# Scattering the token rows themselves into the experts' lists, in place of a list of token numbers

## The chip, the cores and the metric

The kernel runs on one core of a Trainium2 chip. The metric is the device time of one execution in microseconds (us); below it, "the time" is the median of several executions. Engines are named as the profile names them: PE (TensorE, matmuls and transposes), DVE (VectorE), ACT (ScalarE), POOL (GpSimd), SP (SyncE, which here only issues transfers). [...]

## The reference

Three stages follow each other over N = 3072 tokens of width 512 (4 batches of 768 positions, 8 heads of 64):

```python
a = softmax(where(sink(4 keys) | window(128), q @ k.T / 8, -1e9))      # per batch and head
x = (a @ v) regrouped to [3072, 512]
e = argmax(x @ w_gate + modality_bias[modality_id])                     # one of 8 experts a token
y[t] = softmax(...)[e] * (relu(x[t] @ w1[e]) @ w2[e])                   # w1[e] 512x1024, w2[e] 1024x512
out = max(y @ m_w1, y @ m_w2, y @ m_w3) @ m_wo                          # dense, hidden width 768
```

All arithmetic is float32; products are made from a high and a low part (three matmuls for each product of the second and third stage).

## The kernel before

**Attention, 24 blocks of 128 tokens.** The function `beat(g)` writes one eighth of a block's steady state: block n, beat h of 8. The order of every engine's instructions is the order in which they are written; each engine runs its own list in order, and an instruction whose inputs are not ready holds up all that stand behind it on the same engine. In each second beat PE transposes the probabilities of two heads (`flip_p`, L464), ACT copies them to `pT` (L469), POOL cuts them with two selects into `pc` and `pb` (`part_p`, L480), and four beats later PE multiplies them with v (`av`, L513 and L517). So POOL stands on PE's way, with some beats of slack.

**Routing.** Two blocks later the row of x is complete; block n - 3 is routed in beat h = 3 of block n. `place` (L605) works out on DVE the place of each of the 128 tokens in its expert's list (`rowi`: expert number times 3072 plus rank) and POOL scatters the 128 token numbers, 4 bytes each, to these places of the DRAM list `ids` (L617). `store` (L592) puts the gate's factor in column 512 of x (the token number is in column 513, L542) and SP stores the 128 rows of 2056 bytes in token order to the DRAM tensor `xd` (L597). The two chains are woven on DVE, one instruction of each in turn. Every scatter writes `ids` at places that are not known when the program is made, so each waits until the one before it has landed, and every gather of `ids` waits for the last scatter.

**Slots.** The experts' work is cut into slots of 256 tokens of one expert, two halves x of 128 each. The first four slots are chosen from the counts while attention is running (`pick`, L682, one instruction or two a beat; `DONE` = 16, 18, 20, 22 blocks done); the rest are laid out by `tables` (L740) once all counts are known, its steps spread over slot 1, with one large product on POOL (`dots`, L792). A slot's tokens come in two steps: `tokens` (L817) gathers 128 token numbers from `ids` by `idxi` into `tk`, and when these have landed `rows` (L824) gathers the 128 rows of `xd` by `tk` into `xgt`. Both are issued by POOL. For the picked slots `tokens` stands at the end of `pick`; later ones are gathered just ahead of `rows`. Then PE transposes `xgt` (`flip_slot`, L857), multiplies with w1 (L876), ACT and DVE make `hh`, `hl`, and PE multiplies with w2 (L925). Weights come in two tiles of 512 KB by SP each; ACT and DVE split them (`whi` L845, `wlo` L848). `keep_down` (L929) scales the product on DVE into `ytl`, and POOL scatters 128 rows of 2052 bytes to `yd` (L932), each again waiting for the one before.

**Filling work in the slots.** The dense stage's weights arrive as float64 and are converted on DVE in eight steps (`convert`, L639) with a sum on POOL (L663); the next conversion's first step (L647) overwrites what this sum reads.

**Tail and dense stage.** Slots from number 11 on (`tail_slot`, L1345, `last_slot`, L1377) stand under run-time conditions and use `grid`, `masks` and the two `ytl` tiles as scratch (L913), so that ACT waits there until the scatters out of `ytl` have landed. The dense stage (L1464, L1480) follows and keeps PE alone busy.

POOL's list at the end of attention and in slot 1, in order: scatter of block 21, scatter of block 22, `tokens(3)`, first `yd` scatter of slot 0, `rows(2)`, scatter of block 23, second `yd` scatter, `rows(3)`, `dots`, the `yd` scatters of slot 1. In a later slot: two `meta` copies, `tokens`, `rows`, a conversion's sum and store, the two `yd` scatters.

Of the kernel before, what the change touches and what calls it, by code (L numbers as in the profile page):

```python
# [9 lines left out]
F32 = mybir.dt.float32  # L10
F32R = mybir.dt.float32r
BF16 = mybir.dt.bfloat16
I32 = mybir.dt.int32
# [6 lines left out]
P = 128  # L20
# [22 lines left out]
def kernel(  # L43
# [32 lines left out]
    cst = ctx.enter_context(tc.tile_pool(name="cst", bufs=1))  # L76
    drm = ctx.enter_context(tc.tile_pool(name="drm", bufs=1, space=DRAM))

    xd = drm.tile([NT, DM + 2], F32, name="xd")
    yd = drm.tile([NT + SLOT, DM + 1], F32, name="yd")  # L80
    ids = drm.tile([E * NT, 1], I32, name="ids")
    xg = drm.tile([B, S, H, D], F32, name="xg")
    wa = drm.tile([JC, P, 3 * CC * P], F32, name="wa")
    wb = drm.tile([JC, P, DM], F32, name="wb")
# [2 lines left out]
    def iota(shape, pattern, base, mult, name):  # L87
        t = cst.tile(shape, F32, name=name)
        nc.gpsimd.iota(t, pattern=pattern, base=base, channel_multiplier=mult, allow_small_or_imprecise_dtypes=True)
        return t  # L90
# [10 lines left out]
    xgt = [wp.tile([P, DM + 2], F32, name=f"xgt{x}") for x in range(2)]  # L101
    ytl = [wp.tile([P, DM + 1], F32, name=f"ytl{x}") for x in range(2)]
    meta = [[wp.tile([P, 2], F32, name=f"meta{u}{x}") for x in range(2)] for u in range(2)]
    tk = [[wp.tile([P, 1], I32, name=f"tk{u}{x}") for x in range(2)] for u in range(2)]
    xh = wp.tile([P, CC, SLOT], F32R, name="xh")
    xl = wp.tile([P, CC, SLOT], F32R, name="xl")
    hh = wp.tile([P, FC, SLOT], F32R, name="hh")
# [186 lines left out]
        additive_p(mk1, tb[:, 0:4])  # L294

    ltri = cst.tile([P, P], BF16, name="ltri")
    tokid = cst.tile([P, NTILE], I32, name="tokid")
    tokf = cst.tile([P, NTILE], F32, name="tokf")
    zid = mn.tile([P, E * NT // P], I32, name="zid", bufs=1)
    vr = mn.tile([P, B, D], F32, name="vr", bufs=1)  # L300
    bmask = mn.tile([P, H, D], F32, name="bmask", bufs=1)
    prow = cst.tile([P, 1], I32, name="prow")
# [289 lines left out]
    def store(n):  # L592
        s = st[n]
        nc.vector.tensor_scalar(s.gs, s.gs, 1.0e-9, None, ALU.add)
        yield
        nc.vector.reciprocal(s.x[:, DM:DM + 1], s.gs)
        nc.sync.dma_start(xd[n * P:(n + 1) * P, :], s.x)  # L597

    def rank(n):
        s = st[n]  # L600
# [4 lines left out]
    def place(n):  # L605
        s = st[n]
        pos = lt.tile([P, E], F32, name="pos", tag="pos")
        row = lt.tile([P, 1], F32, name="row", tag="row")
        nc.vector.tensor_add(pos, s.pr[:, 0, :], cnt)
        yield  # L610
        nc.vector.tensor_tensor_reduce(
            out=pos, in0=pos, in1=s.oh, scale=1.0, scalar=0.0, op0=ALU.mult, op1=ALU.add, accum_out=row,
        )
        nc.vector.tensor_add(cnt, cnt, s.pr[:, 1, :])
        yield
        nc.vector.tensor_copy(rowi[:, n:n + 1], row)
        nc.gpsimd.indirect_dma_start(  # L617
            out=ids, out_offset=bass.IndirectOffsetOnAxis(ap=rowi[:, n:n + 1], axis=0),
            in_=tokid[:, n:n + 1], in_offset=None,
        )  # L620


    cv = {}
# [58 lines left out]
    def pick(z):  # L682

        c, t = pick_t
        m, w, o = pick_s
        V = nc.vector
        V.tensor_tensor(c, cnt, base_e, ALU.subtract)
        if z:
            V.tensor_tensor(c, c, taken, ALU.subtract)
        yield  # L690
        V.reduce_max(m, c, axis=AX.X)
        yield
        V.scalar_tensor_tensor(t, c, m, wdesc, ALU.is_ge, ALU.mult)
        yield
        V.reduce_max(w, t, axis=AX.X)
        yield
        V.tensor_scalar(pick_oh[z], t, w, None, ALU.is_equal)
        V.tensor_scalar(w, w, -1.0, float(E), ALU.mult, ALU.add)
        yield
        V.tensor_copy(esi[:, z:z + 1], w)  # L700
        V.tensor_scalar(w, w, float(NT), pcol, ALU.mult, ALU.add)
        if z:
            V.tensor_tensor_reduce(
                out=t, in0=taken, in1=pick_oh[z], scale=1.0, scalar=0.0, op0=ALU.mult, op1=ALU.add, accum_out=o
            )
        yield
        if z:
            V.tensor_add(w, w, o)
            yield
        V.tensor_copy(idxi[:, z, 0:1], w)  # L710
        V.tensor_scalar(idxi[:, z, 1:2], w, float(P), None, ALU.add)
        if z:
            V.scalar_tensor_tensor(taken, pick_oh[z], float(SLOT), taken, ALU.mult, ALU.add)
        else:
            V.tensor_scalar(taken, pick_oh[z], float(SLOT), None, ALU.mult)
        for x in range(2):
            yield
            tokens(z, x)

    E2 = 2 * E  # L720
    cnt_e = cst.tile([P, E], F32, name="cnt_e")
# [18 lines left out]
    def tables():  # L740
# [62 lines left out]
        for x in range(2):  # L803
            if x:
                V.tensor_scalar(seff, seff, float(P), None, ALU.add)
            V.tensor_add(idx[:, :, x], dot[:, :, 1], seff)
            V.scalar_tensor_tensor(pos2[:, :, x], dot[:, :, 2], float(PICKS * SLOT), seff, ALU.add, ALU.add)
            V.tensor_tensor(padi[:, :, x], seff, dot[:, :, 3], ALU.is_ge)
        V.tensor_copy(idxi[:, PICKS:, :], idx)
        yield  # L810

        for x in range(2):
            V.tensor_scalar(padi[:, :, x], padi[:, :, x], padn[:, x:x + 1], None, ALU.mult)
        V.tensor_tensor(pos2, pos2, padi, ALU.max)
        V.tensor_copy(posi[:, PICKS:, :], pos2)

    def tokens(s, *only):  # L817
        for x in only or range(2):
            nc.gpsimd.indirect_dma_start(
                out=tk[s % 2][x], out_offset=None, in_=ids,  # L820
                in_offset=bass.IndirectOffsetOnAxis(ap=idxi[:, s, x:x + 1], axis=0),
            )

    def rows(s, upto=None, only=(0, 1)):  # L824
        for x in only:
            nc.gpsimd.indirect_dma_start(
                out=xgt[x], out_offset=None, in_=xd[0:upto] if upto else xd,
                in_offset=bass.IndirectOffsetOnAxis(ap=tk[s % 2][x], axis=0),
            )

    def fetch(s, half, only=range(4)):
# [105 lines left out]
    def weave(*chains):  # L937

        chains = list(chains)
        first = chains[0] if chains else None  # L940
        todo = 0
        while chains:
            todo %= len(chains)
            if next(chains[todo], chains) is chains:
                chains.pop(todo)
            else:
                todo = 0 if todo == 1 and chains[0] is first else todo + 1
# [21 lines left out]
    def beat(g):  # L969
# [63 lines left out]
            if 0 <= c < NCV and x == min(t * CVG // 8, CVG - 1):  # L1033
                chains.append(once(convert, c, t, cvt[c % 2], nc.sync))
        if gone and h == 3:
            chains += [place(n - 3), store(n - 3)]
        if sunk and h == 1:
            chains.append(sink_split(n - 1))
        if prev and h == 4:
# [16 lines left out]
    if True:  # L1056
# [16 lines left out]
        nc.gpsimd.affine_select(  # L1073
            out=ltri, in_=ltri, pattern=[[1, P]], compare_op=ALU.is_gt, fill=0.0, base=0, channel_multiplier=-1
        )
        nc.gpsimd.memset(zid, 0)
        nc.gpsimd.dma_start(ids.rearrange("(p n) o -> p (n o)", p=P), zid)
        nc.gpsimd.iota(prow, pattern=[[0, 1]], base=0, channel_multiplier=1)
        nc.gpsimd.iota(
            bmask, pattern=[[1, H], [0, D]], base=0, channel_multiplier=0, allow_small_or_imprecise_dtypes=True  # L1080
# [2 lines left out]
        base_e = iota([P, E], [[NT, E]], 0, 0, "base_e")  # L1083
        pcol = iota([P, 1], [[0, 1]], 0, 1, "pcol")
        padn = iota([P, 2], [[P, 2]], NT, 1, "padn")
        siota = iota([P, RS], [[1, RS]], 0, 0, "siota")
        kiota = iota([P, SMIN], [[SLOT, SMIN]], 0, 0, "kiota")
        nc.gpsimd.iota(tokid, pattern=[[P, NTILE]], base=0, channel_multiplier=1)
        nc.gpsimd.iota(
            tokf, pattern=[[P, NTILE]], base=0, channel_multiplier=1, allow_small_or_imprecise_dtypes=True  # L1090
        )
# [17 lines left out]
        for g in range(LAST + 1):  # L1109
            beat(g)  # L1110
            n, h = divmod(g, H)
            for z in range(PICKS):
                if n == DONE[z] + 2 and h == 6 + (z == 0):
                    picking.append(pick(z))
            if picking and next(picking[-1], 0) == 0:
                picking.pop()
            if (n, h) in FIRST:
                fetch(0, 0, (FIRST.index((n, h)),))
            if n == DONE[0] + 4 and h in (5, 7):
                rows(0, DONE[0] * P, (h // 2 - 2,))  # L1120

            if (n, h) in HI:
                split_hi(*piece(HI.index((n, h))))
            if (n, h) in LO:
                x = LO.index((n, h))
                split_lo(*piece(x), eng=None if x % 4 else nc.gpsimd.tensor_sub)
            if n == 23:
                if h in (0, 2):
                    px[h // 2] = flip_slot(0, h // 2, ps_tr, "tr")
                if h in (1, 3):  # L1130
                    keep_slot(h // 2, px[h // 2])
                    keep_slot_lo(h // 2, px[h // 2])
                if h == 6:
                    rows(1, DONE[1] * P)
                if h == 7:
                    fetch(1, 0)
    mctx.close()
# [63 lines left out]
    keep_down(0, py, meta[0][0], posi[:, 0, 0:1])  # L1201
    py = ps_av.tile([P, DM], F32, name="py", tag="av")
    down(1, 0, py, lambda: rank(n - 1))
    rows(2, DONE[2] * P)
    split_lo(2)
    split_hi(3)
    weave(place(n - 1), store(n - 1))
    split_lo(3)
    down(1, 1, py)
    keep_down(1, py, meta[0][1], posi[:, 0, 1:2])  # L1210
# [74 lines left out]
    def next_rows(s):  # L1285

        px = [flip_slot(s, x, ps_x, "px") for x in range(2)]
        for x in range(2):
            keep_slot(x, px[x])
            keep_slot_lo(x, px[x])  # L1290
        if s >= SMIN - 1:
            for x in range(2):
                nc.gpsimd.tensor_copy(metal[x], meta[s % 2][x])
            nc.gpsimd.tensor_copy(posl, posi[:, s, :])
        if s + 1 < SMAX:
            if s + 1 >= PICKS:
                tokens(s + 1)
            rows(s + 1)

    def slot(s):  # L1300
# [21 lines left out]
        if s + 1 >= SMIN - 1:  # L1322
            for x in range(2):
                nc.gpsimd.tensor_copy(metal[x], meta[(s + 1) % 2][x])
            nc.gpsimd.tensor_copy(posl, posi[:, s + 1, :])
        if s + 2 >= PICKS:
            tokens(s + 2)
        rows(s + 2)
        for x in range(2):
            py = ps_y.tile([P, DM], F32, name="py", tag="py")  # L1330
# [226 lines left out]
```

## Time and profile before

| | |
|---|---|
| time, median of 3 runs | 1054.43 us (1048.15 to 1061.04) |
| the profiled execution | 1054.27 us, span 1052.7 us, mean granted clock 0.973 |
| PE busy | 994.5 us (94% of the span) |
| DVE busy | 583.2 us (55%) |
| ACT busy | 395.9 us (38%) |
| POOL busy | 322.3 us (31%) |
| hardware queue of SP and ACT | 111.68 MB, 43.1% of the DMA engines' span |
| POOL's own queue | 25.08 MB, 7.1% |

Busy time is an average over four stages: attention to about 290 us, a passage into the slots to about 345 us, slots to about 560 us, the tail to about 640 us, and the dense stage. Matmuls are pipelined and their ends are modelled, so a PE that is shown busy throughout can still run at less than its rate; its real pace is read from the starts of successive instructions. A number in square brackets behind a row of the timeline is the idle time of the engine before this instruction, with the event that the profile holds to have ended it.

### The profile page before, as it was taken

To read this page: it belongs to the slowest core of one execution; us is meant where nothing else is said; L and a number is where in the kernel's file an instruction comes from. 1 tells how busy PE (TensorE), PEld (TensorE's weight loads), DVE (VectorE), ACT (ScalarE), POOL (GpSimd) and SP (SyncE) were. 2 spreads that over 40 slices of the span, in tenths; PEclk is the share of its full clock that TensorE was granted. 3 is DMA by queue.
4 is the path that set the end of the run, shared out by engine and by line. 5 is a ranking of instruction groups with operands and counts; after the bars stand their busy time and mean duration, and the time that the engine had idled before them with its cause. 6 is when DMAs were issued, how large, how long until landed. Compare 5 with 4: busy or idle time off the path is not lost. (4 is left out here: it accounts for less than half of the span.)

```text
span 1052.7 us, 16293 instructions
## 1 busy us (share of the span) xinstructions
PE 994.5 (94%) x5621; PEld 857.2 (81%) x5621; DVE 583.2 (55%) x1312; ACT 395.9 (38%) x974; POOL 322.3 (31%) x503
## 2 busy tenths in 40 slices
PE   6998999998998999989999779999999999999997
PEld 4898988987887998979988657888888888888885
DVE  3787886886767897969898354512302213122120
ACT  3665564565553444434445343411111111111111
POOL 4444434435525454434555450010010000100001
PEclk8998998999999999999999889999999999999999
DMA  7494999666478889787988544210100101100001
GB/s 148 108 123 103 155 124 140 141 118 144 95 205 239 258 293 286 231 283 224 312 262 297 180 135 140 90 50 21 31 40 21 41 21 31 50 13 18 30 1 41
DMA packets 134081, 137.96 MB, mean 131 GB/s; under 512 B 85888, under 2 KB 95248, under 8 KB 133984
## 3 DMA queue, kind: packets, MB, share of 16 engines
q1 hardware_dynamic: 124464, 111.68, 43.1%
q0 software_dynamic: 9376, 25.08, 7.1%
q8 instruction: 49, 0.80, 0.3%
q14 instruction: 48, 0.39, 0.2%
q10 hardware_dynamic: 144, 0.00, 0.0%
HBM read 117.19 MB, written 25.87 MB: 136 GB/s over the span
## 5 line engine op out<-in xcount | busy, mean ns | idle before, releaser
L1464 PE MATMUL pa<-yh,wah 128*128 128x512 f32 x432 | 170.9, 396 | 0.0
L1464 PE MATMUL pa<-yh,wal 128*128 128x512 f32 x432 | 169.9, 393 | 0.0
L1464 PE MATMUL pa<-yl,wah 128*128 128x512 f32 x432 | 169.6, 393 | 0.0
L848 DVE TENSOR_TENSOR wlo<-wraw,whi 128x1024 fp32r<-128x1024 f32 (+1 forms) x110 | 143.8, 1314 | 13.3 <-ACT whi L845 12.9
L1469 DVE TENSOR_TENSOR mm<-pa,mm 128x512 f32<-128x512 f32 x36 | 24.9, 691 | 193.2 <-PE pa L1464 193.2
L845 ACT CAST whi<-wraw 128x1024 fp32r<-128x1024 f32 (+1 forms) x116 | 114.3, 1022 | 21.8 <-PE py L925 17.3
L876 PE MATMUL ph<-xh,wlo 128*128 128x256 f32 x352 | 102.2, 290 | 6.1 <-DVE wlo L848 6.1
L426 PE MATMUL sc<-kT,qz 128*128 128x260 f32 (+1 forms) x384 | 102.3, 391 | 4.8 <-POOL qz L359 3.7
L876 PE MATMUL ph<-xh,whi 128*128 128x256 f32 x352 | 101.5, 288 | 0.0
L876 PE MATMUL ph<-xl,whi 128*128 128x256 f32 x352 | 101.4, 288 | 0.0
L1471 ACT CAST dh<-mm 128x512 fp32r<-128x512 f32 x36 | 22.4, 621 | 197.7 <-DVE mm L1470 197.7
L1464 PEld LDWEIGHTS pa<-yh,wal 128*128 128x128 f32 x432 | 81.1, 188 | 18.4
L1464 PEld LDWEIGHTS pa<-yl,wah 128*128 128x128 f32 x432 | 81.2, 188 | 17.9
L1464 PEld LDWEIGHTS pa<-yh,wah 128*128 128x128 f32 x432 | 81.1, 188 | 17.7
L1484 POOL DMA_INDIRECT out_dram<-ot,ti x24 | 23.3, 973 | 207.7 <-ACT ot L1483 207.7
L925 PE MATMUL py<-whi,hh 128*128 128x512 f32 x208 | 84.5, 406 | 0.7 <-DVE hl L904 0.3
L925 PE MATMUL py<-whi,hl 128*128 128x512 f32 x208 | 82.1, 395 | 0.0
L925 PE MATMUL py<-wlo,hh 128*128 128x512 f32 x208 | 82.0, 394 | 0.0
L426 PEld LDWEIGHTS sc<-kT,qz 128*128 128x128 f32 x384 | 67.8, 200 | 12.0 <-POOL qz L359 4.2
L452 ACT ACTIVATE pp<-sc,m 128x132 f32<-128x132 f32 (+1 forms) x192 | 70.6, 372 | 11.4 <-DVE m L445 10.7
L876 PEld LDWEIGHTS ph<-xh,wlo 128*128 128x128 f32 x352 | 68.3, 194 | 6.8 <-DVE wlo L848 6.8
L513 PE MATMUL av<-vn,pb 128*128 128x64 f32 x320 | 60.0, 270 | 11.0 <-POOL pb L480 8.6
(269 smaller groups left out, 2095.8 us busy)
## 6 DMA issues: line engine op xcount, KB each, us to landing
wraw<-in_moe_w_dram SPq DMA_DIRECT2D x119, 512.0 KB
xd<-x SPq DMA_DIRECT2D x24, 257.0 KB
yn<-yd SPq DMA_DIRECT2D x24, 256.5 KB
kn<-in_k_dram SPq DMA_DIRECT2D x24, 256.0 KB
qn<-in_q_dram SPq DMA_DIRECT2D x24, 256.0 KB
vn<-in_v_dram SPq DMA_DIRECT2D x24, 256.0 KB
x<-xg ACTq DMA_DIRECT2D x24, 256.0 KB
cvr<-in_moe_w_dram SPq DMA_DIRECT2D x11, 512.0 KB
```

What stands on the lines that cost most here:

```text
L426: nc.tensor.matmul(ps[:, o, :w], s.qT[:, h + o, :], kT[:, c, a:a + w], start=True, stop=True)
L452: nc.scalar.activation(s.p[:, h, :w], s.sc[h // 2][:, h % 2, :w], AF.Exp, bias=s.m[:, h:h + 1], scale=1.0, accum_out=s.sum[:, h:h + 1],)
L513: nc.tensor.matmul(s.av[:, h, :], back_p[:, h % 2], st[n - 1].v[:, h, :], start=(h == 0), stop=False, skip_group_check=True,)
L845: (eng or nc.scalar.copy)(whi[c][:, o], wraw[c][:, o])
L848: (eng or nc.vector.tensor_sub)(wlo[c][:, o], wraw[c][:, o], whi[c][:, o].bitcast(F32))
L876: nc.tensor.matmul(ph[:, g, :], a[:, fs], m[:, c, :], start=(n == 0 and g == 0), stop=(n == 3 * CC - 1), skip_group_check=True,)
L925: nc.tensor.matmul(py, a[:, f, hs], m[:, ws], start=(f == 0 and i == 0), stop=(f == FC - 1 and i == 2))
L1464: nc.tensor.matmul(ps, a[:, sl], m[:, c, :], start=(n == 0), stop=(n == 3 * CC - 1))
L1469: nc.vector.tensor_tensor(m, pa[1], m, ALU.max)
L1471: nc.scalar.copy(dh[:, j, :], m)
L1484: nc.gpsimd.indirect_dma_start(out=out, out_offset=bass.IndirectOffsetOnAxis(ap=ti[g % 2][:, t:t + 1], axis=0), in_=o, in_offset=None,)
```

## The change

Rows of x no longer lie in `xd` in token order. `xd` grows to 24576 rows of 514 words (8 lists of 3072), and POOL scatters each block's 128 rows of 2056 bytes straight to `rowi`, in place of SP's store. The list `ids`, its zeroing at the start, its scatter, the tiles `tk` and every gather of `tokens` are gone; `rows` gathers from `xd` by `idxi`. `place` and `store` are one chain, `place_store`, so the scatter stands behind the reciprocal. Since the rows now read all of `xd`, the bounds that `rows` had (only the blocks that are done) are gone; `rows(0)` moves from beats 5 and 7 of block 20 to beats 0 and 2 of block 21. The list's unused places hold nothing now, so `tables` sends the indices of a slot's missing tokens back to its first row, with two more DVE instructions and one more step. Block 22's place is worked out where it was, but its scatter stands where its store stood, behind the end of `pick(3)`.

```diff
-    xd = drm.tile([NT, DM + 2], F32, name="xd")
+    xd = drm.tile([E * NT, DM + 2], I32, name="xd")
-    ids = drm.tile([E * NT, 1], I32, name="ids")
...
         nc.vector.reciprocal(s.x[:, DM:DM + 1], s.gs)
-        nc.sync.dma_start(xd[n * P:(n + 1) * P, :], s.x)
+        nc.gpsimd.indirect_dma_start(
+            out=xd, out_offset=bass.IndirectOffsetOnAxis(ap=rowi[:, n:n + 1], axis=0),
+            in_=s.x.bitcast(I32), in_offset=None,
+        )
...
         nc.vector.tensor_copy(rowi[:, n:n + 1], row)
-        nc.gpsimd.indirect_dma_start(
-            out=ids, out_offset=bass.IndirectOffsetOnAxis(ap=rowi[:, n:n + 1], axis=0),
-            in_=tokid[:, n:n + 1], in_offset=None,
-        )
+
+    def place_store(n):
+        yield from place(n)
+        yield
+        yield from store(n)
...
-        for x in range(2):
-            yield
-            tokens(z, x)
...
+        yield
+
+        for x in range(2):
+            V.scalar_tensor_tensor(
+                idx[:, :, x], padi[:, :, x], back[:, x:x + 1], idx[:, :, x], ALU.mult, ALU.add
+            )
         V.tensor_copy(idxi[:, PICKS:, :], idx)
...
-    def tokens(s, *only):
-        for x in only or range(2):
-            nc.gpsimd.indirect_dma_start(
-                out=tk[s % 2][x], out_offset=None, in_=ids,
-                in_offset=bass.IndirectOffsetOnAxis(ap=idxi[:, s, x:x + 1], axis=0),
-            )
-
-    def rows(s, upto=None, only=(0, 1)):
+    def rows(s, only=(0, 1)):
         for x in only:
             nc.gpsimd.indirect_dma_start(
-                out=xgt[x], out_offset=None, in_=xd[0:upto] if upto else xd,
-                in_offset=bass.IndirectOffsetOnAxis(ap=tk[s % 2][x], axis=0),
+                out=xgt[x].bitcast(I32), out_offset=None, in_=xd,
+                in_offset=bass.IndirectOffsetOnAxis(ap=idxi[:, s, x:x + 1], axis=0),
             )
...
         if gone and h == 3:
-            chains += [place(n - 3), store(n - 3)]
+            chains.append(place_store(n - 3))
...
-        nc.gpsimd.memset(zid, 0)
-        nc.gpsimd.dma_start(ids.rearrange("(p n) o -> p (n o)", p=P), zid)
...
+        back = iota([P, 2], [[-P, 2]], 0, -1, "back")
...
-            if n == DONE[0] + 4 and h in (5, 7):
-                rows(0, DONE[0] * P, (h // 2 - 2,))
+            if n == DONE[0] + 5 and h in (0, 2):
+                rows(0, (h // 2,))
...
-    weave(place(n - 1), store(n - 1))
+    weave(place_store(n - 1))
...
         if s + 1 < SMAX:
-            if s + 1 >= PICKS:
-                tokens(s + 1)
             rows(s + 1)
...
-        if s + 2 >= PICKS:
-            tokens(s + 2)
         rows(s + 2)
```

## Rows read from the trace of the kernel before

**Rows 1.** Busy time by stage: PE, PEld, DVE, ACT, POOL, clock, DMA share, GB/s.

```profile
345.00:560.00 215.00, 207.42 (x1351) 190.45 (x1350) 186.31 (x263) 99.40 (x131) 100.61 (x113) 0.98 0.84 266
560.00:640.00 80.00, 68.31 (x294) 52.81 (x293) 43.58 (x47) 34.62 (x45) 38.35 (x47) 0.91 0.56 179
```

**Rows 2.** Waits of all engines: who waited for whom, us in total, times, longest.

```profile
DVE cvt L647 <- POOL cvt L663: 20.3, 5, 8.6
...
POOL vs L370 <- DMA ids<-tokid,rowi: 18.8, 3, 7.8
...
PE av L513 <- POOL pb L480: 8.6, 5, 2.7
```

**Rows 3.** Groups of POOL's instructions: busy us, mean ns | idle before them, what ended it.

```profile
L826 POOL DMA_INDIRECT xgt<-xd,tk x30 | 35.8, 1193 | 55.3 <-DMA tk<-ids,idxi 36.3 <-PE py L925 5.2 <-PE px L1258 4.1
...
L819 POOL DMA_INDIRECT tk<-ids,idxi x30 | 33.3, 1112 | 35.2 <-DVE cnt_e L744 11.6 <-DVE x L596 6.6 <-DMA ids<-tokid,rowi 6.3
```

**Rows 4.** PE's timeline, four of its stalls: start, us, instruction, idle before.

```profile
239.84 0.43 PE L513 MATMUL av<-vn,pb 128*128 128x64 f32 x2 [2.54 <-POOL pb L480]
...
334.22 1.97 PE L857 MATMUL px<-ident,xgt 128*128 128x128 f32 x8 [4.83 <-DMA xgt<-xd,tk]
...
470.69 0.58 PE L876 MATMUL ph<-xh,wlo 128*128 128x256 f32 x1 [3.93 <-DVE wlo L848]
...
583.20 1.11 PE L901 MATMUL px<-ident,ytl 128*128 128x128 f32 x4 [2.78 <-ACT ytl L913]
```

**Rows 5.** PE's timeline: the transposes that begin three successive slots.

```profile
430.51 1.03 PE L857 MATMUL px<-ident,xgt 128*128 128x128 f32 x8
...
453.83 1.04 PE L857 MATMUL px<-ident,xgt 128*128 128x128 f32 x8
...
484.93 1.03 PE L857 MATMUL px<-ident,xgt 128*128 128x128 f32 x8
```

**Rows 6.** Transfers of the page: issuer, number, KB each or median us to landing.

```profile
xd<-x SPq DMA_DIRECT2D x24, 257.0 KB
...
tk<-ids,idxi POOLq DMA_INDIRECT x30, 5.9
xgt<-xd,tk POOLq DMA_INDIRECT x30, 5.6
yd<-ytl,posi POOLq DMA_INDIRECT x25, 7.4
ids<-tokid,rowi POOLq DMA_INDIRECT x24, 8.6
```

**Rows 7.** POOL's timeline in attention: two scatters of successive blocks, a later gather.

```profile
106.46 0.98 POOL L617 DMA_INDIRECT ids<-tokid,rowi  x1 [1.11 <-DVE rs L532]
...
116.86 1.00 POOL L617 DMA_INDIRECT ids<-tokid,rowi  x1 [1.00 <-DVE x L596]
...
238.00 1.01 POOL L819 DMA_INDIRECT tk<-ids,idxi  x1 [6.63 <-DVE x L596]
```

**Rows 8.** The transfers that write or read the list `ids`: us to landing.

```profile
DMA to landing us min/median/max: 2.7/6.6/12.0
```

**Rows 9.** Timelines of DVE and POOL, passage into the slots.

```profile
308.65 0.16 DVE L596 RECIPROCAL x<-gs 128x1 f32<-128x1 f32 x1
...
320.34 1.02 POOL L819 DMA_INDIRECT tk<-ids,idxi  x1 [11.58 <-DVE cnt_e L744]
...
327.60 0.95 POOL L826 DMA_INDIRECT xgt<-xd,tk  x1 [0.30 <-DMA tk<-ids,idxi]
...
340.49 3.18 POOL L792 TENSOR_TENSOR dots<-here,vec 128x960 f32<-128x960 f32 x1 [2.12 <-DVE vec L791]
```

**Rows 10.** Timelines of DVE, POOL and ACT at the head of the tail.

```profile
565.51 0.75 DVE L930 TENSOR_SCALAR ytl<-py,meta 128x512 f32<-128x512 f32 x1
...
574.88 1.01 POOL L932 DMA_INDIRECT yd<-ytl,posi  x1 [0.28 <-POOL ytl L931]
...
582.55 0.60 ACT L913 ACTIVATE ytl<-ph 128x512 f32<-128x512 f32 x1 [5.66 <-DMA wb<-cvt]
```

More of the change, by code (lines that the diff above doesn't have):

```diff
@@ L103 @@
     meta = [[wp.tile([P, 2], F32, name=f"meta{u}{x}") for x in range(2)] for u in range(2)]
-    tk = [[wp.tile([P, 1], I32, name=f"tk{u}{x}") for x in range(2)] for u in range(2)]
     xh = wp.tile([P, CC, SLOT], F32R, name="xh")
@@ L296 @@
     ltri = cst.tile([P, P], BF16, name="ltri")
-    tokid = cst.tile([P, NTILE], I32, name="tokid")
     tokf = cst.tile([P, NTILE], F32, name="tokf")
-    zid = mn.tile([P, E * NT // P], I32, name="zid", bufs=1)
     vr = mn.tile([P, B, D], F32, name="vr", bufs=1)
@@ L1085 @@
         padn = iota([P, 2], [[P, 2]], NT, 1, "padn")
+        back = iota([P, 2], [[-P, 2]], 0, -1, "back")
         siota = iota([P, RS], [[1, RS]], 0, 0, "siota")
         kiota = iota([P, SMIN], [[SLOT, SMIN]], 0, 0, "kiota")
-        nc.gpsimd.iota(tokid, pattern=[[P, NTILE]], base=0, channel_multiplier=1)
         nc.gpsimd.iota(
@@ L1133 @@
                 if h == 6:
-                    rows(1, DONE[1] * P)
+                    rows(1)
                 if h == 7:
@@ L1203 @@
     down(1, 0, py, lambda: rank(n - 1))
-    rows(2, DONE[2] * P)
+    rows(2)
     split_lo(2)
     split_hi(3)
-    weave(place(n - 1), store(n - 1))
+    weave(place_store(n - 1))
     split_lo(3)
```

## The prediction

> **What bounds the kernel now.** I read the stages first, then who waits for whom, then the timelines of PE and POOL around PE's stalls. PE is busy for nearly all of attention and of the dense stage; in the slots it is busy for 207.4 of 215.0 us and in the tail for 68.3 of 80.0 [rows 1]. So PE sets the end, and a change to POOL, SP and their transfers can only be worth the time in which PE stands still because of them. The dense stage knows neither `ids` nor `xd` and is left as it is.
>
> The list costs POOL twice. Its 30 gathers take 33.3 us to issue and 35.2 us of idling before them; the gathers of rows idle 36.3 us for the token numbers to land [rows 3]. POOL's list is in order, so whatever stands behind waits too: the selects of attention, the sums of the conversions, the scatters to `yd`. The question for each is whether PE notices. PE's timeline says yes in four places [rows 4]. At 239.84 it waits 2.54 us for POOL's selects, which stand behind the gather at 238.00 and its 6.63 us of idling [rows 7]; the row names DVE's reciprocal as the releaser, on which that gather does not depend, so it was the scatter before it. At 334.22 it waits 4.83 us for the rows of slot 2. At 470.69 it waits 3.93 us for a split of DVE: DVE had waited up to 8.6 us for POOL's sum [rows 2], which stands behind the rows that wait for their token numbers. At 583.20 it waits 2.78 us for ACT, which waits for a scatter out of `ytl`: DVE filled the tile at 565.51, POOL scattered it only at 574.88, and ACT could go on at 582.55 [rows 10].
>
> **The change, part by part.** The sum is made against the profiled execution, 1054.27 us, which stands at the median of the runs, 1054.43.
>
> *The scatter of a block.* There are 24 scatters before and after; each takes POOL 1.0 us to issue with 4 bytes a row [rows 7], and the nearest rows with 2056 bytes, the gathers, take 1.19 [rows 3]: at most 0.2 us a block, beside a POOL that idles in every block, so nothing. SP loses 24 stores of 257 KB [rows 6]; the same bytes now go through POOL's queue, so the transfer engines have as much to do, and I count nothing. What matters is when the scatter has landed, because the next one waits for that. Blocks follow each other 10.40 us apart, and the scatter at 116.86 idled 1.00 us, again put to a reciprocal that it doesn't need, so it was waiting for the scatter before [rows 7]. This chain is all but tight. The lower bound for a heavier scatter is below nothing: `yd`'s, with 2052 bytes a row, lands in 7.4 us, the list's in 8.6. Also between gathers the payload costs nothing, 5.6 us against 5.9 [rows 6]. The upper bound is the longest landing of the list, 12.0 us [rows 8]. The nearest rows are the two gathers, equal but for the payload; I take 0.5 us later, which the selects' slack mostly covers, and charge 1.5 us for attention, between 0 and 7. That the scatter now stands behind the reciprocal adds three short DVE instructions in the same beat, nothing while it waits for its forerunner anyway.
>
> [...]
>
> *Gathers of token numbers in attention.* Six of the 30 go. PE's five waits for the selects come to 8.6 us [rows 2]; the longest, 2.7, stands at the end of attention before `rows(1)`, which still waits for the scatter of three beats before, so it stays, and another follows POOL's instruction L370, which waits for a scatter with or without the change. I take off 4 us. New are two waits: `rows(0)` for the scatter five beats before (some 6.5 us, by then nearly landed: 1 or 2 us), and the scatter of block 18, one beat behind `rows(0)`, for that gather's 5.6 us. Behind both stand selects. The like wait at 238.00 was 6.63 us and cost PE 2.54; this one is some 4.5, and I charge 1. Attention gains 3, less the 1.5 above.
>
> *Passage into the slots.* Today POOL reaches `rows(2)` late: it idles 11.58 us until 320.34 before the gather of `tokens(3)`, for block 22's scatter to land, and issues the second half of `rows(2)` at 327.60 [rows 9]; PE stalls at 334.22. In the new order the scatter of block 22 is issued behind the reciprocal at 308.65 and lands near 321 by the same delay, and `rows(2)`, directly behind, go at 322 and 323, some 4 to 5 us earlier. PE's 4.83 us are then nearly gone, and with them the lower clock after the stall: the eight transposes took 1.97 us against 1.04 [rows 4, 5]. That is 6 us. Against it: block 23's scatter now waits for `rows(2)` to have read `xd` (issued near 331, landed near 339), `rows(3)` wait for it, and `dots` stands behind them at some 343 where it stood at 340.49 [rows 9]. DVE waits for `dots`, and so falls some 6 us back against a PE that is 5 ahead. I leave 2 us for that: 4 us gained. The two added DVE instructions of `tables` run once and vanish in the same wait.
>
> *Slots.* The 22 gathers of slots 4 to 14 and their waits leave POOL's list, so that the sums of the conversions come some 6 us earlier. A slot without a stall takes 453.83 - 430.51 = 23.3 us, the one that holds the stall at 470.69 takes 484.93 - 453.83 = 31.1 [rows 5]: 7.8 us, of which I take 7.5. The other four of DVE's five waits, 11.7 us in all [rows 2], cost PE little, as PE is shown busy for all but 7.6 us of the 215 [rows 1]: 1 us. DVE, busy for 186.3 of 215 us, has room to follow. Together 8.5. At the least it is nothing, if DVE or the weights (DMA share 0.84) hold the slots up instead.
>
> *Tail.* The first scatter of `ytl` can follow at about 566.6 what it followed at 574.88 [rows 10], 8 us earlier than ACT's 5.66 us of waiting asks for. PE's 2.78 us go, the half clock behind them, and part of a similar stall behind the second `ytl`: 6 us, of 11.7 in which PE is idle there [rows 1], bounds 2 and 9.
>
> *Start.* Zeroing the list and one index table go, one small table comes; POOL has more than a microsecond less to do before its first select, which waits for ACT: nothing.
>
> The sum: 3 - 1.5 + 4 + 8.5 + 6 = 20 us; 1054.3 - 20 = 1034.
>
> **The rivals.** *The waits move and most of the gain is lost.* Scatters into `yd` still wait for each other in POOL's list, and rows of x still wait for the last scatter. If DVE falls behind because of `dots`, and the slots are held by DVE or by the weights, the passage gives 1, the slots 4, the tail 3 and attention 0: 1046. For it speaks DVE at 87% of the slots; against it the 23.3 us slots, in which PE is not held up by anything. *Slower: the scatters' chain becomes the pace of attention.* Place: the wait of every scatter for the one before. It decides once a landing passes about 10 us, since blocks come every 10.4. If the heavier scatter lands in 11.1 us, 2.5 later and still under the 12.0 seen, each wait grows by 1.5 to 2 us with selects behind it, and 21 blocks lose about 31 us: 1054 + 31 - 20 = 1065. For it speaks the 1.00 us of idling in rows 7 and the 18.8 us that L370 waits for scatters [rows 2]; against it that payload has no price in rows 6. *More than forecast.* If the heavier scatter lands as `yd`'s does, 1.2 us sooner, the chain loosens, L370's waits shrink, and with the whole of the slots' and the tail's idle time gone it is 1022.
>
> **How the numbers follow.** Chances: the forecast 0.54, the moved waits 0.24, slower 0.10, more than forecast 0.12. About 1% (10.5 us) is what a measurement can tell from no change. Faster by more than that is the forecast, the last case and little else: 0.66. Within 1% is nearly all of the moved waits and the edges of the neighbours: 0.25. Slower: 0.09. The forecast alone has 1026 to 1043, from the bounds of slots and tail; the range, 1021 to 1053, takes in the moved waits and the larger gain and leaves out slower.
>
> **What would show it.** No wait of POOL for `tk`; PE's stall at the rows of slot 2 under 1.5 us; no wait of DVE at L647 above 2 us; ACT's wait at L913 gone at the head of the tail; the x scatter's median landing between 8 and 9.5 us, and PE's waits for the selects under 6 us in all. The prediction is wrong if that landing passes 10 us, if PE stalls in slot 2 behind DVE and `dots`, or if slots without a stall become longer than 23.3 us.

## The result and the profile after

The changed kernel takes 1009.03 us (median of 4 runs, 1007.24 to 1012.21) where the kernel before took 1051.72 beside it: a ratio of 0.9584 (95% interval 0.9514 to 0.9655), 42.7 us less. The forecast was 1034 and its range 1021 to 1053, so the result lies outside the range: the forecast was right in sign, and its 20 us are less than half of the gain. The profiled execution took 1008.41 us.

The page's head for the changed kernel; the columns are busy us, share of the span and number of instructions of each engine.

```profile
span 1006.9 us, 16226 instructions
## 1 busy us (share of the span) xinstructions
PE 977.8 (97%) x5621; PEld 844.7 (84%) x5621; DVE 575.8 (57%) x1314; ACT 395.5 (39%) x974; POOL 285.9 (28%) x471
```

PE's busy time fell by 16.7 us, the span by 45.8: some 29 us of it is time in which PE stood still. Where it went is read from three marks in PE's timeline: the first transposes of slot 3 and of slot 11, and the first matmul of the dense stage (640.13 before, 595.50 after). All kernels of this document but e5 and e6 (at each mark within 1.7 us of e7), in us; the right part is the difference of the marks. Each row is one execution, so a difference of a microsecond or two in it is no finding.

| kernel | slot 3 | slot 11 | dense | to slot 3 | slots 3 to 10 | tail |
|---|---|---|---|---|---|---|
| before | 359.1 | 557.8 | 640.1 | 359.1 | 198.7 | 82.3 |
| after | 334.2 | 523.4 | 595.5 | 334.2 | 189.2 | 72.1 |
| e1 list kept | 351.3 | 540.2 | 612.5 | 351.3 | 188.9 | 72.3 |
| e2 store kept | 332.3 | 520.8 | 593.4 | 332.3 | 188.5 | 72.6 |
| e3 before, L370 on DVE | 358.3 | 555.2 | 640.5 | 358.3 | 196.9 | 85.3 |
| e4 before, tokens early | 356.2 | 549.2 | 623.6 | 356.2 | 193.0 | 74.4 |
| e7 list kept, 512 bytes apart | 335.2 | 524.6 | 595.5 | 335.2 | 189.4 | 70.9 |
| e8 list kept, L367 on DVE | 355.1 | 544.5 | 617.2 | 355.1 | 189.4 | 72.7 |
| e9 before, list apart | 334.1 | 525.0 | 607.3 | 334.1 | 190.9 | 82.3 |
| e10 before, apart and early | 332.7 | 524.0 | 596.9 | 332.7 | 191.3 | 72.9 |
| e11 gathers added | 335.9 | 524.6 | 597.3 | 335.9 | 188.7 | 72.7 |
| e12 list by SP | 385.8 | 575.6 | 647.2 | 385.8 | 189.8 | 71.6 |

The first two rows give 24.9 us of gain up to slot 3, 9.5 in the slots, 10.2 in the tail, together 44.6. The prediction had 5.5, 8.5 and 6. The surprise is attention with the passage.

What is different there is the transfers. The stretch from 60 to 240 us in both kernels, before and then after; the columns are those of [rows 1] (the last three: TensorE's granted clock as a share of the full one, busy share of the DMA engines, GB/s).

```profile
60.00:240.00 180.00, 168.82 (x1218) 155.65 (x1217) 144.93 (x500) 103.99 (x417) 79.73 (x152) 0.94 0.81 131
```

```profile
60.00:240.00 180.00, 173.11 (x1297) 159.98 (x1296) 150.56 (x526) 109.73 (x441) 87.12 (x165) 0.98 0.59 142
```

More bytes move in less of the engines' time. And the scatter lands much sooner. The landing times of transfers that touch the list (before) and `xd` (after), from 40 to 240 us; the second holds five of the 18 scatters, those whose landing the trace has.

```profile
DMA to landing us min/median/max: 3.8/8.9/12.0
```

```profile
DMA to landing us min/median/max: 3.1/3.6/4.8
```

So the scatter with 514 times the bytes lands, in these five, in less than half the time. The waits after that answer to [rows 2]: POOL's subtraction after the scatter (L370, now L367), the conversion (L647, now L648), and PE's waits of `av`, none of which is for POOL's selects now.

```profile
PE av L514 <- DVE x L538: 3.3, 3, 1.2
...
DVE cvt L648 <- POOL cvt L664: 6.5, 3, 4.2
POOL vs L367 <- DMA xd<-x,rowi: 4.0, 2, 2.3
...
PE av L510 <- DVE x L538: 0.8, 2, 0.5
```

PE at the rows of slots 2 and 3 has no stall (4.83 us in [rows 4]), and the slots follow each other in 23.3 us:

```profile
310.92 1.04 PE L853 MATMUL px<-ident,xgt 128*128 128x128 f32 x8
...
334.23 1.04 PE L853 MATMUL px<-ident,xgt 128*128 128x128 f32 x8
357.52 1.04 PE L853 MATMUL px<-ident,xgt 128*128 128x128 f32 x8
```

Stretches that answer to [rows 1], the slots and the tail: PE is idle for 1.3 and 6.2 us of them, where it was 7.6 and 11.7.

```profile
320.00:525.50 205.50, 204.22 (x1351) 188.06 (x1350) 186.41 (x265) 99.31 (x131) 79.74 (x99) 1.00 0.86 283
525.50:595.50 70.00, 63.80 (x294) 50.57 (x293) 41.26 (x47) 34.73 (x45) 33.05 (x41) 0.95 0.61 201
```

### The profile page after: what moved, and what is told of

Same layout as the page of the kernel before. It is cut to its first block, busy times and chain, and to the rows that moved or that the text cites. A ratio compares the mean times of both kernels' runs of the same rounds, so it can differ in the third digit from the quotient of the medians.

```text
span 1006.9 us, 16226 instructions
## 1 busy us (share of the span) xinstructions
PE 977.8 (97%) x5621; PEld 844.7 (84%) x5621; DVE 575.8 (57%) x1314; ACT 395.5 (39%) x974; POOL 285.9 (28%) x471
## 5 line engine op out<-in xcount | busy, mean ns | idle before, releaser
L844 DVE TENSOR_TENSOR wlo<-wraw,whi 128x1024 fp32r<-128x1024 f32 (+1 forms) x110 | 135.7, 1241 | 15.2 <-ACT whi L841 14.4
L1459 DVE TENSOR_TENSOR mm<-pa,mm 128x512 f32<-128x512 f32 x36 | 24.9, 691 | 193.4 <-PE pa L1454 193.4
L872 PE MATMUL ph<-xh,wlo 128*128 128x256 f32 x352 | 99.6, 283 | 0.0
L872 PEld LDWEIGHTS ph<-xl,whi 128*128 128x128 f32 x352 | 67.5, 192 | 0.4
L872 PEld LDWEIGHTS ph<-xh,whi 128*128 128x128 f32 x352 | 67.5, 192 | 0.4
```

The lines of the kernel that those rows point to most:

```text
L844: (eng or nc.vector.tensor_sub)(wlo[c][:, o], wraw[c][:, o], whi[c][:, o].bitcast(F32))
L872: nc.tensor.matmul(ph[:, g, :], a[:, fs], m[:, c, :], start=(n == 0 and g == 0), stop=(n == 3 * CC - 1), skip_group_check=True,)
L1459: nc.vector.tensor_tensor(m, pa[1], m, ALU.max)
```

## The experiments

Each was timed in turns with the kernel before on the same chip. There the kernel before took 1051.89 us (e1 to e4), 1055.59 (e5 to e8), 1068.31 (e9 to e11) and 1075.46 (e12). The four series ran on four chips, and the changed kernel itself was timed in none of them: a time that is set against its 1009.03 us is compared across series, a ratio is not.

### Which transfer was slow: e1 and e2

e1 adds the old list's scatter behind the new one, e2 adds SP's old store, both into tensors that nobody reads.

```diff
 # e1, behind the scatter of x
+        nc.gpsimd.indirect_dma_start(
+            out=ids, out_offset=bass.IndirectOffsetOnAxis(ap=rowi[:, n:n + 1], axis=0),
+            in_=tokid[:, n:n + 1], in_offset=None,
+        )
 # e2, ahead of it
+        nc.sync.dma_start(xs[n * P:(n + 1) * P, :], s.x)
```

> The changed kernel, to which the old list's scatter is added again: behind each block's scatter of x, POOL also scatters 128 token numbers of 4 bytes into a list of its own, which nobody reads. Theory A (the 4-byte scatter was the slow transfer, and what waited for it, POOL's L370 (now L367) and the next scatter, paced attention): it lands in 8 to 10 us as before, L367 waits some 15 to 20 us in its three or four places again, the blocks take 11 us and more, the packets of q, k and v are held up for microseconds, and the end comes 12 to 18 us later than the changed kernel, 1021 to 1027. Theory B (the slow landing belonged to SP's direct store of x, which shared the engines with it): the list's scatter lands in 3 to 5 us, one more POOL instruction of 1.0 us a block vanishes in its idle time, 1009 to 1012.

> The changed kernel, to which SP's direct store of each block's 257 KB of x into a tensor in token order is added again (nobody reads it). Theory A (the list's 4-byte scatter was the slow transfer): the scatter of x still lands in 3 to 5 us and the time stays at 1008 to 1012. Theory B (the store was): landings of 7 to 10 us return, L367 waits for them, and attention ends 10 to 18 us later, 1019 to 1027.

e1 took 1024.65 us (ratio 0.973, 0.9691 to 0.9769), e2 1007.03 (0.9558, 0.9518 to 0.9599): Theory A in both. SP's store of 257 KB a block costs nothing; the list's 512 bytes a block cost 15.6 us, and by the table all of it before slot 3. The landing of e1's list scatter, from 40 to 240 us as above, and the stretch from 60 to 240:

```profile
DMA to landing us min/median/max: 6.2/8.9/11.1
```

```profile
60.00:240.00 180.00, 167.72 (x1245) 153.68 (x1244) 152.16 (x509) 105.42 (x424) 99.75 (x172) 0.98 0.73 131
```

The scatter of x in front of it in the same queue has slowed down too, to a median of 7.9 (3.3 to 10.3). In e2 the transfers that touch `xd` land in 3.4 to 6.5 us with a median of 5.5, later than the 3 to 5 that Theory A gave, and the time does not show it. The waits of e1 that came back (L369 is L367 of the changed kernel):

```profile
POOL xgt L828 <- DMA xd<-x,rowi: 15.6, 4, 6.1
POOL vs L369 <- DMA ids<-tokid,rowi: 14.3, 2, 8.1
...
PE av L512 <- POOL pb L479: 9.7, 7, 3.0
```

### What makes it slow: e5, e6 and e7

e5 and e6 scatter 64 and 512 bytes a row of x in place of the 4-byte number; e7 keeps 4 bytes, but puts the words 512 bytes apart.

```diff
 # e5 (16 words) and e6 (128 words), against e1
-            in_=tokid[:, n:n + 1], in_offset=None,
+            in_=s.x[:, 0:16].bitcast(I32), in_offset=None,
 # e7, against e1
+        nc.vector.tensor_scalar(rowl[:, n:n + 1], row, 128.0, None, ALU.mult)
-            out=ids, out_offset=bass.IndirectOffsetOnAxis(ap=rowi[:, n:n + 1], axis=0),
+            out=ids, out_offset=bass.IndirectOffsetOnAxis(ap=rowl[:, n:n + 1], axis=0),
```

> The changed kernel with a second scatter of each block as in the experiment that kept the list, but with 64 bytes a row (the first 16 numbers of the token's x) in place of 4; nobody reads it. Theory S (any second scatter a block costs this): 1022 to 1027, landings 8 us and more. Theory P (what is slow is the row of 4 bytes, or rows that lie 4 bytes apart): lands in 3 to 6 us, 1008 to 1013.

> The same with 512 bytes a row. Theory S: 1022 to 1027. Theory P: 1008 to 1013. If the bytes of a row set it gradually, this lies between the run with 64 bytes and the changed kernel's 1009.

> The changed kernel with the 4-byte list scatter of the first experiment, but the rows of its list lie 512 bytes apart (one short DVE instruction a block multiplies the row numbers). Theory P1 (a write of 4 bytes is slow by itself): 1022 to 1027, landings 8 to 10 us. Theory P2 (it is slow because some 16 tokens of a block go to neighbouring words for each expert, so that writes of 4 bytes meet in the same few bytes of memory): landings 3 to 5 us, 1008 to 1013.

They took 1009.82, 1010.68 and 1010.43 us (ratios 0.9571, 0.9576, 0.9581, each within 0.003): all like the changed kernel. So neither a second scatter is slow nor the 4 bytes by themselves, but 4-byte writes side by side. The traces of the three hold no landing of these scatters; POOL's wait for the second scatter, 14.3 us in e1, is 3.1, 2.5 and 2.6 us. e7's stretch from 60 to 240 us has the share and rate of the changed kernel:

```profile
60.00:240.00 180.00, 172.13 (x1302) 159.50 (x1302) 154.61 (x545) 111.08 (x444) 106.30 (x182) 0.99 0.59 141
```

The size alone does not decide here: e7 writes 4 bytes at a time like e1, and took 14.2 us less (1010.43 against 1024.65, across series; 15.7 less than the 1026.09 of e8 below, which has e1's list in e7's series).

### Whether it reaches PE by the wait behind it: e3 and e8

The instruction that waits longest for the list, the subtraction of `sink_values`, goes from POOL to DVE: in the kernel before (e3) and in e1 (e8).

```diff
-            nc.gpsimd.tensor_sub(vs4[b][hf], vx[hf], vs4[b][hf].bitcast(F32))
+            nc.vector.tensor_sub(vs4[b][hf], vx[hf], vs4[b][hf].bitcast(F32))
```

> The kernel before with one instruction of POOL moved: the subtraction of L370 (four times in the kernel), which waits for the list's scatter just issued, runs on DVE, where it does not. Theory A1 (L370's 18.8 us of waiting reach PE through the selects behind it): PE's waits for the selects near 97, 163 and 293 us go, with the half clock behind them, and the kernel gains 8 to 13 us, 1039 to 1044. Theory A2 (the chain of landings paces the blocks whether or not L370 waits; the next scatter waits instead): under 4 us, 1048 to 1052.

> The changed kernel with the 4-byte list scatter added as in the first experiment, and POOL's subtraction L367, the one that waits for it (14.3 us in two places there), moved to DVE. If that wait is the way in which the slow landing reaches PE, some 6 to 9 us of the 15.6 come back: 1016 to 1019. If the slow landings reach PE by other ways (the scatter and the gathers of rows that wait for them, loads held up), under 3 us: 1022 to 1026.

e3 took 1052.27 us (0.9989, 0.9955 to 1.0022), e8 1026.09 (0.9717, 0.9685 to 0.9748): nothing gained in either. In e3 the first transposes of slot 0 came 5.1 us earlier (266.7 against 271.8), and PE then waited 5.6 us in two stalls for slot 2's rows, where the kernel before had waited 4.83 [rows 4]; at slot 3 less than 1 us of the lead was left:

```profile
329.68 0.66 PE L857 MATMUL px<-ident,xgt 128*128 128x128 f32 x4 [3.19 <-DMA xgt<-xd,tk]
...
332.72 1.12 PE L857 MATMUL px<-ident,xgt 128*128 128x128 f32 x4 [2.38 <-DMA xgt<-xd,tk]
```

In e8 hardly anything waits for the list any more; this is all that its trace shows under who waited for it:

```profile
who waited for it (us, times):
  POOL ids L600: 1.0, 1
```

and 17 us are lost all the same. So it is not by instructions that wait for the list that the time is lost.

### By what it reaches PE: e12

SP writes 128 words side by side for each block. POOL's queue has none of it, and no instruction waits for it.

```diff
+    ids = drm.tile([NT, 1], I32, name="ids")
...
+        nc.sync.dma_start(ids[n * P:(n + 1) * P, :], tokid[:, n:n + 1])
```

> The changed kernel, in which SP, not POOL, writes each block's 128 token numbers of 4 bytes, side by side in token order, into a tensor that nobody reads: no index, nothing in POOL's queue, and no instruction waits for it. Theory E (neighbouring 4-byte writes hold up whatever else the transfer engines carry, the loads and the scatter of x among it): the packets of the loads get slower, the scatters of x land in 6 us and more, and it costs 8 to 16 us, 1017 to 1025. Theory Q (they only hold up what stands behind them in POOL's queue): under 2 us, 1007 to 1011.

1057.11 us: 48 us over the changed kernel's 1009.03, for 24 transfers of 512 bytes (ratio to the kernel before 0.9841, 0.9799 to 0.9883; that one took 1075.46 here). Theory E holds, at some three times the most that I gave it; by the table all of the loss, 51.6 us, comes before slot 3. The size of 48 us is a comparison across chips, since no kernel without such writes was timed in this series; in the other three such kernels took 1007 to 1014 us, the cured e9 below apart. The trace has no landing of the scatters of x; POOL's subtraction (L369 here) waits for them 21.7 us in three places, 4.0 in the changed kernel. The stretch from 60 to 240 us: the transfer engines are busy throughout and move less.

```profile
60.00:240.00 180.00, 162.25 (x1154) 150.20 (x1153) 136.13 (x465) 97.08 (x392) 72.86 (x139) 0.93 0.97 117
```

PE then waits for whatever came late: behind ACT for a load of x, and behind POOL's selects, which stand behind a scatter that waits for the gather of rows issued at 276.88 to land. The load is in ACT's queue, the gather in POOL's, the writes are in SP's. Two of PE's stalls in its timeline, then the instruction of ACT and of POOL behind which each arose:

```profile
257.42 0.47 PE L463 MATMUL pt<-ident,pp 128*128 128x128 f32 x1 [7.42 <-ACT pp L451]
...
290.18 0.69 PE L512 MATMUL av<-vn,pb 128*128 128x64 f32 x2 [8.72 <-POOL pb L479]
```

```profile
256.90 0.37 ACT L451 ACTIVATE pp<-sc,m 128x132 f32<-128x132 f32 x1 [8.00 <-DMA x<-xg]
```

```profile
276.88 0.96 POOL L825 DMA_INDIRECT xgt<-xd,idxi  x1 [0.16 <-issue]
...
288.33 1.00 POOL L596 DMA_INDIRECT xd<-x,rowi  x1 [9.71 <-DMA xgt<-xd,idxi]
```

That other queues pay can also be read from the pages of e1 and e7, which differ in the list's layout and in one short DVE instruction a block. The list is in POOL's queue; the queue of SP and ACT carries the same packets and bytes in both (packets, MB, share of the span of 16 engines; e1, then e7):

```profile
q1 hardware_dynamic: 121008, 105.36, 41.1%
```

```profile
q1 hardware_dynamic: 121008, 105.36, 37.1%
```

That is 41.1% of 1021.6 us against 37.1% of 1008.5, 46 us more of the engines' time for the same transfers. So the slow writes held up other transfers, loads and scatters alike: these 46 us, the 8.00 us that ACT waited for a load in e12 (such a wait stands nowhere in the changed kernel's trace), and the 7.9 us to landing of e1's scatter of x (3.6 in the changed kernel). In e12 they were late in other queues than the writes'; by what mechanism no run shows.

### The kernel before, cured: e9 and e10

e9 is the kernel before with its list spread out, 64 bytes from word to word; all its scatters, gathers and waits stay. e10 also gathers the token numbers of a slot at the end of the slot before, which e4 does by itself.

```diff
 # e9 (and e10)
-    ids = drm.tile([E * NT, 1], I32, name="ids")
+    ids = drm.tile([E * NT * 16, 1], I32, name="ids")
-        nc.vector.tensor_copy(rowi[:, n:n + 1], row)
+        nc.vector.tensor_scalar(rowi[:, n:n + 1], row, 16.0, None, ALU.mult)
...
 # e4 (and e10): slot(s), and next_rows likewise
-        if s + 2 >= PICKS:
-            tokens(s + 2)
         rows(s + 2)
...
+        if s + 3 < SMAX:
+            tokens(s + 3)
```

> The kernel before, complete, with nothing changed but that the words of its list lie 64 bytes apart (the row numbers and the list indices are multiplied by 16, the zeroing covers 16 times as much; every scatter, gather and wait stays). Theory N (what cost attention was neighbouring 4-byte writes): the list's scatters land in 3 to 5 us instead of 8.9, POOL's L370 waits little for them, and the kernel gains 13 to 18 us, 1035 to 1042; the slots keep their stalls. Theory L (the list costs attention by its instructions and waits as such, or 64 bytes are not far enough): under 4 us, 1050 to 1056.

> The kernel before, in which the token numbers of slots 4 to 15 are gathered at the end of the slot before, some 15 us ahead of the rows that need them: the list, its scatters and its gathers all stay, only POOL's wait for a token gather that has just been issued goes. If these waits are what slots and tail lost (8.5 and 6 us in the prediction, some 9.5 and 10 in the comparison of the traces), it gains 14 to 20 us: 1032 to 1038. If the 1.1 us of issuing each gather and what the queue carries matter as much, it gains half of that, 1042 to 1046; if the slots' and tail's gain came down from attention (other phases of the clock, buffers freed earlier), under 4 us.

> The last kernel, and the token numbers of slots 4 to 15 gathered a slot early as well, so that the list is kept, but neither its layout nor the wait for a gather just issued costs anything. If the two parts add (15.6 and 10 to 13 us), it gains 25 to 29 us, 1024 to 1030, and what is left to the changed kernel, some 15 us, is the price of the list's other instructions and of attention's and the passage's token gathers. If both are the same loss seen twice, 1035 to 1040.

e9 took 1022.14 us beside 1068.31 (0.9561, 0.9506 to 0.9617): 46.2 us less where Theory N gave 13 to 18. Some of that belongs to this series' slower kernel before; against the traced one, which took 1054.27 us, the mark of the dense stage is 32.9 us earlier. Up to slot 3 it runs like the changed kernel, 334.1 against 334.2, with POOL's gathers and waits for token numbers all in place, L370's wait down to 3.6 us and the stretch as it is after the change:

```profile
POOL vs L370 <- DMA ids<-tokid,rowi: 3.6, 2, 2.3
```

```profile
60.00:240.00 180.00, 173.76 (x1295) 161.09 (x1294) 150.62 (x521) 109.62 (x437) 88.38 (x167) 0.97 0.59 139
```

What stays is the tail, 82.3 us as before. That is what e4 takes away: 1041.71 us (0.9898, 0.986 to 0.9936), 10.2 us less. The traced executions lie 16.0 us apart, more than the medians; by their marks 7.9 us are gained in the tail and 5.7 in the slots. I had expected 14 to 20, with the wait gone. It is not gone: in POOL's list the gathers now stand behind the last scatter of the slot before, but still only shortly ahead of the rows that need them. POOL's waits for token numbers before it gathers rows, in the slots of the kernel before (345 to 560 us) and then in e4 (345 to 640, with none left in the tail):

```profile
POOL xgt L826 <- DMA tk<-ids,idxi: 29.1, 7, 6.6
```

```profile
POOL xgt L826 <- DMA tk<-ids,idxi: 22.7, 6, 5.9
```

e10 has both and took 1014.03 us beside 1068.31 (0.949, 0.9437 to 0.9542), 10 us below the range that I expected. It is 5.0 us over the changed kernel's median, and by its marks 1.4 us behind it: nearly the whole gain without moving a row of x.

### The gathers without the wait: e11

```diff
+        if s + 2 >= PICKS:
+            tokens(s + 2)
         rows(s + 2)
```

> The changed kernel with the 4-byte token gathers of slots 4 to 15 issued again in their old places, out of a list of zeros, for nobody: POOL has 24 more instructions of 1.1 us and the queue 24 more gathers, but no instruction waits for their numbers. If issuing and carrying them is what slots and tail lost beside the waits, it costs 4 to 7 us: 1013 to 1017. If only the waits were it, under 2 us: 1008 to 1011.

1011.33 us (0.9453, 0.9399 to 0.9507), 2.3 over the changed kernel's median and just over the 1008 to 1011 of the second case. From slot 3 to the dense stage, where the added gathers are, it takes 261.4 us against 261.3: issuing and carrying them costs nothing there, which leaves the wait for their numbers.

## Why the prediction was wrong, point by point

**What bounds the kernel** held: PE sets the end, and the dense stage is unchanged. Some 29 us of the gain were PE's stalls, and 16.7 a shorter busy time of the same 5621 instructions, at a granted clock of 0.992 in place of 0.973. So did the sign.

**The step that failed is "The scatter of a block".** It had SP's bytes move to POOL's queue, "so the transfer engines have as much to do", priced the scatter by its payload (0.5 us later, 1.5 us lost), and took the list's 8.6 us for what such a scatter costs. The runs show the opposite: the list's own writes were slow, because some 16 numbers of a block go side by side for each expert, and they made other transfers slow. No run shows the 0.5 us, the 1.5 charged for it or the upper bound of 7: the scatter of x landed in 3.6 us where the list's transfers took 8.9 (medians from 40 to 240 us). The true term is a gain, 24.9 us up to slot 3 in the trace (e9 gives 25.0 by the layout alone). Put back into the changed kernel, the same writes cost 17.1 there (e1); that the kernel before lost more may come from its gathers that wait for the list, which no run separates. A sign stood in the profile of the kernel before and I did not read it: the slots move 266 GB/s at a busy share of 0.84 [rows 1], attention needed 0.81 for 131, twice the engine time for a byte. Not all of that was the list, since attention still needs 1.4 times the slots' after the change (0.59 for 142 against 0.86 for 283); but it called for a cause, and the odd transfer there was the one of 4 bytes a row. Pricing a write by gathers, which read, was the wrong nearest row.

**Gathers of token numbers in attention**, 3 us: attention did gain, but not by this cause. e9 keeps these gathers and is as fast up to slot 3. PE's waits that I put down to them were the late list. L370, which I had keep its wait "with or without the change", fell from 18.8 to 4.0 us, since what it waits for lands sooner; yet e3 and e8 show that its wait is not a lever either.

**Passage**, 4 us: from slot 1 to slot 3 it took 54.8 us before (304.3 to 359.1) and 48.2 after (286.0 to 334.2), 6.6 less, where the forecast had 6 less 2. But e9 has the old order and the same 48.2, so it was again the landings and not the order.

**Slots**, 8.5 us: 9.5 measured. The mechanism was right in part: e4, which only shortens POOL's waits, gains 5.7, and in the changed kernel DVE's waits at L647 went from 20.3 to 6.5 us in all. But e9 alone gains 7.8, and e10, with both, 7.4: the two overlap. Whether in e9 the shorter waits for numbers (at most 4.5 us instead of 6.6) or another phase against DVE's work does it, no run separates.

**Tail**, 6 us with bounds 2 and 9: 10.2 measured. The mechanism holds: no wait of ACT for a scatter out of `ytl` at L909 is left; e9 leaves the tail as it was, and e4 gives 7.9 of it.

**What I had named to look for.** Right: no wait for `tk` (which is gone by the change itself), no stall of PE at the rows of slot 2, the slots at 23.3 us, ACT's wait gone, no wait of PE for the selects. Wrong: the landing (8 to 9.5 us forecast, 3.6 measured), and DVE still waits up to 4.2 us for POOL's sum without PE noticing.

**The rivals.** The moved waits did not come: the slots stay at 23.3 us. The slower case needed a landing of 10 us or more; it was 3.6. "More than forecast" named the right thing, a chain that loosens because the scatter lands sooner, but took 1.2 us sooner from `yd`'s scatters where it was 5.3, and got 0.12 and 1022.

## What to carry to other kernels

Before costing a transfer by its bytes, set the busy share of the DMA engines against the GB/s in two stages: here 0.81 at 131 GB/s in the kernel before, against 0.59 at 142 in the changed one (both from 60 to 240 us), meant that something held the engines up, and in e12 (0.97 at 117) that was writes for which no instruction waits. The share by itself is a sign and not a price: e2 has 0.70 at 165 GB/s in that stretch and takes 1007.03 us, the changed kernel 1009.03. Here 24 scatters of 512 bytes in small words side by side cost 15.6 us (e1), and 24 stores of 257 KB nothing (e2); spread such words, or write whole rows. And where removing a wait gains nothing, as in e3, look for what was late for all of them.

## What the hardware showed beyond that

Writes of 4 bytes side by side cost 0.65 us of the whole kernel for each scatter of 128 in e1 (15.6 / 24), and some 2.0 us in e12 (48.1 / 24, across chips), where all 128 stand in one row and SP writes them; with 64 bytes or more from word to word (e9: slot 3 at 334.1 us, in the changed kernel at 334.2; e7: 1010.43 us in all, against 1009.03), or with rows of 64 bytes back to back (e5: 1009.82), nothing that these runs can tell. Why neighbours are slow no run here shows. The cost also seems to vary with the chip: the kernel before took 1052, 1056, 1068 and 1075 us in the four series, while the kernels without such writes lie between 1007 and 1014 in the three that had one, the cured e9 apart, whose tail keeps its waits.
